# Fused attention and two expert layers on one core: scores and probabilities x values of neighbouring tiles in one group on TensorE, the eight transposes in another, in turns 8 to 21

## Chip, cores and metric

The kernel runs on one core of a Trainium2 chip. The metric is the time of one execution in device microseconds, as the median of three runs. Engines are written as the profile writes them: PE is TensorE (matmuls; a transpose is a matmul with the identity matrix), PEld its weight loads, DVE VectorE, ACT ScalarE, POOL GpSimd, SP SyncE, which here only issues transfers.

## What is computed

The reference has three parts, one behind the other:

```python
# attention: 4 batches x 8 heads, 768 tokens, 64 per head; chunks of 32 tokens
# that look at 8 memory keys and 16 tokens to the left, 8 to the right
scores = scale * np.matmul(q_c, k_full.transpose(0, 1, 3, 2))
a = np.exp(scores - np.max(scores, axis=-1, keepdims=True))
a = a / (np.sum(a, axis=-1, keepdims=True) + 1e-09)
out[:, :, c_start:c_end] = np.matmul(a, v_full)
# layer 1: x is 3072 x 512, w_in 512 x 1024, w_out 1024 x 512
h = x @ w_in
e = np.exp(h - h_max); sm = e / (np.sum(e, axis=-1, keepdims=True) + 1e-9)
solu = h * sm
ln = (solu - mu) / np.sqrt(var + 1e-06) * g_ln
x2 = ln @ w_out
# layer 2: 512 -> 2048 -> 512
h = x2 @ w_in2; g = np.maximum(0.01 * h, h); return g @ w_out2
```

Weights come as 64-bit floats and are decoded on the chip. Products of layer 1 are made of three: each operand is split into a high and a low half (names that end in `h` and `l`), and high x high, high x low and low x high are added up.

## The kernel before

The 3072 tokens are 24 tiles of 128. After a start written out by hand the loop from line 477 runs turns i = 0 to 24; behind it comes layer 2 (line 715 and around it), which the change leaves as it is. A turn works on several tiles at once, at different stages:

- **Attention of tile a = i + 2.** `s_scores` (S): 16 matmuls of 128x32 column groups (line 208) into a PSUM tile `att`; each such group shows as 32 instructions in the trace. Then the negated row maxima `nms` on DVE (lines 217, 218; in the first and the last tile of a batch a memset ahead). `s_exp`: eight exponentials on ACT (line 225), one a head, into `p`. `s_pt` (PT): four transposes of `p` (line 238) into a PSUM tile `tr`, copied out by DVE as `pt` (line 242). `s_pv` (PV): 16 matmuls probabilities x values (line 250) into another `att`, scaled out by DVE as `x` (line 255). `x_halves` (XT): four transposes of `x` (line 264), then `xh` on ACT (line 267) and `xl` on DVE (line 270).
- **Layer 1, first half, of tile i.** `s_h`: 24 matmuls "h" (line 284) of 128x512 into PSUM `h`, then a chain between DVE and ACT: `hnm` (DVE, line 297), `e` (ACT, the exponential of line 300), `hrs` (DVE, 301 and 302), `so` and `nmu` (DVE, 305 and 308), the square (ACT, line 310), `ve` (DVE 311), `rstd` (POOL 313) and the normalized `so` (DVE 318).
- **Its transposition, of tile i - 1.** `s_lt` in turns 7 to 22: two DVE transposes of 32x32 blocks into `sl` (line 337), a store to DRAM (`lnd`, SP's queue), four loads back issued by ACT (`lt`, line 346), and two copies each on ACT and DVE into the halves `lhl` (lines 354, 355).
- **Layer 1, second half, of tile i - 5.** `s_o`: 24 matmuls of 128x512 into PSUM `x2p` (line 366, "products" below), copied out by ACT as `x2s` (line 374) and stored by ACT's queue. Turn 7 takes three blocks.
- **Decoding of layer 2's weights** from turn 9 on: per turn one `abs` on ACT (line 112), four steps on DVE (lines 114 to 127), and every second turn four more DVE operations on `w3s` (lines 470 to 473).

`p` and `x` have one buffer, `att` and `tr` two, `h` one. Except in the start, the order of instructions on each engine is that of the tile framework's scheduler: it places S, PT, PV and XT between the h matmuls and the products where it thinks their inputs are ready. Each engine then runs its own list strictly in that order, and waits at semaphores.

Of the kernel before, what the change touches and what calls it, by code (L numbers as in the profile page):

```python
# [33 lines left out]
ON_POOL = range(6)  # L34

SPARE_PSUM = (1, 3, 5)

F64_LO = struct.unpack("<f", struct.pack("<I", 0x38000000))[0]
F64_HI = struct.unpack("<f", struct.pack("<I", 0x47EFFFFF))[0]
# [3 lines left out]
def tile_kernel(  # L43
# [14 lines left out]
    NTILE = qt.shape[0]  # L58
# [38 lines left out]
    def load_raw(src, pool):  # L97
        raw = pool.tile([P, 512, 2], U32, name="raw")
        if len(src.shape) == 2:
            nc.sync.dma_start(out=raw.rearrange("p f w -> p (f w)"), in_=src)  # L100
        else:
            nc.sync.dma_start(out=raw.rearrange("p (k f) w -> p k (f w)", k=src.shape[1]), in_=src)
        return raw
# [39 lines left out]
    def decode(raw, dh, dl, pool, gain=None, sub=nc.gpsimd):  # L143
        for _ in decode_steps(raw, dh, dl, gain, pool, sub):
            pass
        return lows[-1]
# [24 lines left out]
    def kv_tile(pool, name, eng):  # L171
        t = pool.tile([P, 2, 4, 4, 64], F32, name=name)
        eng.memset(t[:, 0], 0.0)
        eng.memset(t[:, 1], 0.0)
        return t
# [3 lines left out]
    kbd = kv_tile(p1, "kbd", nc.vector)  # L179
    vbd = kv_tile(p1, "vbd", nc.vector)  # L180

    def load_q(i):
        q = pa.tile([P, 4, P], F32, name="q")
        nc.sync.dma_start(out=q, in_=qt[i].rearrange("p (h t) -> p h t", h=4))
        return q

    def load_kv(i, dst, src):
        for j in range(2):
            nc.sync.dma_start(
                out=dst[j::2, j], in_=src[i, j::2].rearrange("p (h c k) -> p h c k", h=4, c=4)  # L190
            )
        return dst

    def load_tile(i):
        return load_q(i), load_kv(i, kbd, kw), load_kv(i, vbd, vw)

    def load_w2(kk):
        decode(
            load_raw(w2[kk * P : (kk + 1) * P, :], dec), w2h[:, kk], w2l[:, kk],
            dec, g_sb[:, kk : kk + 1],  # L200
        )

    def s_scores(i, q, k):
        sc = ps_att.tile([P, 8, 64], F32, name="att")
        for hp in range(4):
            for c in range(4):
                cs = slice(32 * c, 32 * c + 32)
                nc.tensor.matmul(  # L208
                    sc[cs, 2 * hp : 2 * hp + 2, :], q[:, hp, cs], k[:, :, hp, c, :],
                    start=True, stop=True,  # L210
                )
        if i % TPB == 0:
            nc.vector.memset(sc[0:32, :, 8:24], NEG)
        if i % TPB == TPB - 1:
            nc.vector.memset(sc[96:128, :, 56:64], NEG)
        nms = sm.tile([P, 8], F32, name="nms")
        nc.vector.tensor_reduce(out=nms, in_=sc, op=ALU.max, axis=AX.X, negate=True)
        nc.vector.tensor_scalar_mul(nms, nms, SCALE)  # L218
        return sc, nms

    def s_exp(sc, nms):
        p = p1.tile([P, 4, 64, 2], F32, name="p")
        rs = sm.tile([P, 8], F32, name="rs")
        for h in range(8):
            nc.scalar.activation(  # L225
                p[:, h // 2, :, h % 2], sc[:, h], AF.Exp, bias=nms[:, h : h + 1], scale=SCALE,
                accum_out=rs[:, h : h + 1],
            )
        return p, rs

    def s_rs(rs):
        nc.vector.tensor_scalar_add(rs, rs, 1e-9)
        nc.vector.reciprocal(rs, rs)

    def s_pt(p):
        ptp = ps_tr.tile([P, 4, P], F32, name="tr")
        for hp in range(4):
            nc.tensor.transpose(  # L238
                ptp[:, hp], p[:, hp].rearrange("p k j -> p (k j)"), ident
            )  # L240
        pt = pa.tile([P, 4, P], F32, name="pt")
        nc.vector.tensor_copy(pt, ptp)
        return pt

    def s_pv(pt, v, rs):
        xp = ps_att.tile([P, 8, 64], F32, name="att")
        for hp in range(4):
            for c in range(4):
                cs = slice(32 * c, 32 * c + 32)
                nc.tensor.matmul(  # L250
                    xp[cs, 2 * hp : 2 * hp + 2, :], pt[:, hp, cs], v[:, :, hp, c, :],
                    start=True, stop=True,
                )
        x = p1.tile([P, 8, 64], F32, name="x")
        nc.vector.tensor_tensor(
            out=x, in0=xp, in1=rs.unsqueeze(2).to_broadcast([P, 8, 64]), op=ALU.mult
        )
        return x

    def s_xt(x):  # L260
        xtp = ps_tr.tile([P, 4, P], F32, name="tr")
        xf = x.rearrange("p h k -> p (h k)")
        for kk in range(KD):
            nc.tensor.transpose(xtp[:, kk], xf[:, kk * P : (kk + 1) * P], ident)  # L264
        xh = pa.tile([P, KD, P], F32R, name="xh", bufs=3)
        xl = pa.tile([P, KD, P], F32R, name="xl", bufs=3)
        nc.scalar.activation(xh, xtp, AF.Copy)

        def low():
            nc.vector.tensor_tensor(out=xl, in0=xtp, in1=xh.bitcast(F32), op=ALU.subtract)  # L270

        return (xh, xl), low

    def x_halves(x):
        hl, low = s_xt(x)
        low()
        return hl
# [122 lines left out]
    ENG = mybir.EngineType  # L400
# [52 lines left out]
    ld = load_tile(3)  # L453
# [7 lines left out]
    def store_w3(f, m):  # L461
        w3m.append(m.bitcast(F32))
        a = m.bitcast(F32).rearrange("p (k f) -> p k f", k=2)
        if f % 2 == 0:
            nc.sync.dma_start(out=w3f[f // 2, :, 0:2], in_=a)
            return
        s = p2.tile([P, 3, 256], F32, name="w3s")
        b = w3m[-2].rearrange("p (k f) -> p k f", k=2)
        tt = nc.vector.tensor_tensor
        tt(out=s[:, 0], in0=a[:, 0], in1=a[:, 1], op=ALU.add)  # L470
        tt(out=a[:, 0], in0=b[:, 0], in1=a[:, 0], op=ALU.subtract)
        tt(out=s[:, 1], in0=s[:, 0], in1=b[:, 0], op=ALU.subtract)
        tt(out=s[:, 2], in0=b[:, 1], in1=s[:, 1], op=ALU.subtract)
        nc.sync.dma_start(out=w3f[f // 2, :, 2:4], in_=a)
        nc.sync.dma_start(out=w3f[f // 2, :, 4:7], in_=s)

    for i in range(NTILE + 1):
        a = i + 2
        b, t = divmod(i, TB)
        if i < NTILE and t == 0:  # L480
            lhl = lp.tile([P, 2, KF, BT], F32R, name="lhl")
            lb[b] = (lhl[:, 0], lhl[:, 1])
        att = 2 < a < NTILE
        if att:
            p, rs = s_exp(*s_scores(a, ld[0], ld[1]))
            s_rs(rs)
        nso = None
        if i == max(SPARE_PSUM) + 1:
            sx2.close()
            ps_x2 = sx2.enter_context(tc.tile_pool(name="ps_x2b", bufs=2, space=PSUM, side="right", reuse_waits="tile"))  # L490
        if i == NTILE - 1:
            sps.close()
            ps_h2 = sps.enter_context(tc.tile_pool(name="ps_h2", bufs=1, space=PSUM, reuse_waits="tile"))
            spare = ps_h2.tile([P, DFF], F32, name="h2")
        if i < NTILE:
            if i < 2:
                nso = s_h(None, hs[i], True)
            else:
                nso = s_h(xs.pop(0), spare if i in (*SPARE_PSUM, NTILE - 1) else None, i in ON_POOL)
        if att:  # L500
            pt = s_pt(p)
        if so is not None:
            j = i - 1
            s_lt(so, j // TB, j % TB, *lb[j // TB])
        so = nso
        if att:
            x = s_pv(pt, ld[2], rs)
            if a + 1 < NTILE:
                ld = load_tile(a + 1)
        for kk in W2_AT.get(i, ()):  # L510
            load_w2(kk)
        if w3s is not None:
            store_w3(i - 1 - W3_FROM, w3s)
        if 0 <= i - W3_FROM < KF2:
            f = i - W3_FROM
            raw = load_raw(w3[:, 2 * f * P : 2 * (f + 1) * P].rearrange("(k p) f -> p k f", p=P), dec)
            w3s = decode(raw, None, None, dec)
        js = O_AT.get(i, (i - LAG,) if i >= LAG else ())
        for j in js:
            s_o(j // TB, j % TB, *lb[j // TB], 0)  # L520
            if att and j == js[0]:
                xs.append(x_halves(x))
            s_o(j // TB, j % TB, *lb[j // TB], 1)
        if att and not js:
            xs.append(x_halves(x))

    store_w3(KF2 - 1, w3s)
    sps.close()
# [497 lines left out]
```

## Time and profile before

| what | us |
|---|---|
| median of three runs | 846.62 (846.52 to 846.77) |
| the profiled execution | 845.34 |
| its span in the trace | 843.6 |
| PE busy in it | 824.1 (98%) |
| turns 8 to 21, from the start of S in turn 8 to that in turn 22's place | 206.5 |

[...] A turn is counted from the start of its S on PE: turn 8 begins at 120.59 us, turn 9 at 140.35, turn 10 at 155.18, and turn 21 ends at 327.13. Turn 8 carries 24 products more; the others are alike. Busy time on PE is that of a pipeline: its matmuls overlap, so what one costs is read from the distance between starts and not from its duration. The granted clock of PE is 1.00 of full speed all through these turns.

### The profile page before, as it was taken

The page shows a single profiled execution, that of the slowest core. Times are in us where ns is not written, and L with a number is a line of the kernel's source. Part 1 is how long each engine was busy: PE and PEld are TensorE (multiplying, and loading weights), DVE is VectorE, ACT ScalarE, POOL GpSimd, SP SyncE. Part 2 cuts the span into 40 slices and gives each one's busy share as a digit, 9 for nine tenths or more (in the row PEclk, how much of TensorE's full clock was granted, in tenths as well). Part 3 has the DMA queues.
Part 4 walks back from the last instruction along what each step waited for, and adds up shares of the span by engine and source line. Part 5 has one row for each costly group of instructions (what it writes and reads, how often), then busy time and mean ns, then how long its engine had stood idle before and what let it go on. Part 6 is the DMA issues. An engine that isn't in the chain of part 4 may idle for free.

```text
span 843.6 us, 13753 instructions
## 1 busy us (share of the span) xinstructions
PE 824.1 (98%) x5014; PEld 663.8 (79%) x5014; DVE 644.6 (76%) x1145; ACT 471.1 (56%) x1067; POOL 57.4 (7%) x63
## 2 busy tenths in 40 slices
PE   7899999999999999999999999999999999999998
PEld 6676777777777778887888888888787888888886
DVE  8989986878787778758888855675689678768663
ACT  5587844554555444537555646677657344544541
POOL 3333300000000000000000000000000000010001
PEclk9999999999999999999999999999999999999999
DMA  9555685877777576532889964586696375546542
GB/s 335 198 179 177 202 282 190 264 256 241 251 245 243 182 218 212 214 139 96 309 324 314 328 251 199 196 324 258 242 364 220 124 267 188 196 160 230 189 148 101
DMA packets 69892, 190.97 MB, mean 226 GB/s; under 512 B 8000, under 2 KB 32064, under 8 KB 65856
## 3 DMA queue, kind: packets, MB, share of 16 engines
q1 hardware_dynamic: 56864, 175.14, 58.9%
q10 hardware_dynamic: 12960, 14.95, 5.5%
q8 instruction: 40, 0.66, 0.3%
q14 instruction: 28, 0.23, 0.1%
HBM read 129.24 MB, written 60.82 MB: 225 GB/s over the span
## 4 chain that ended last, share of the span: by engine, by line
PE 86%; DVE 6%; ACT 4%; DMA 2%; POOL 1%; issue 1%; DVEq 0%; ACTq 0%; SPq 0%; POOLq 0%
PE C L715 25%; PE x2p L366 16%; PE B L715 14%; PE h L284 13%; PE A L715 10%; PE att L250 3%; PE att L208 2%; DMA ring<-gd 1%; PE tr L238 1%; PE tr L264 1%; DVE ring L826 1%; ACT p L225 1%; PE x2p L284 1%; DMA kbd<-in_kw 1%; POOL w2l L138 1%
## 5 line engine op out<-in xcount | busy, mean ns | idle before, releaser
L366 PE MATMUL x2p<-lhl,w2h 128*128 128x512 f32 x384 | 126.7, 406 | 0.0
L715 PE MATMUL C<-xP,L 128*128 128x512 f32 x384 | 95.4, 390 | 2.2 <-ACT u L744 1.7
L715 PEld LDWEIGHTS C<-xP,L 128*128 128x128 f32 x384 | 71.9, 188 | 17.9 <-ACT u L744 2.1
L366 PEld LDWEIGHTS x2p<-lhl,w2h 128*128 128x128 f32 x384 | 69.8, 189 | 16.3 <-issue 2.4
L366 PE MATMUL x2p<-lhl,w2l 128*128 128x512 f32 x192 | 77.6, 404 | 0.0
L225 ACT ACTIVATE p<-att,nms 128x64 f32<-128x64 f32 x192 | 57.6, 328 | 25.3 <-DVE nms L218 25.2
L284 PE MATMUL h<-w1h,xh 128*128 128x512 f32 x168 | 69.3, 412 | 0.0
L284 PE MATMUL h<-w1h,xl 128*128 128x512 f32 x168 | 67.0, 399 | 0.0
L715 PE MATMUL C<-h,L 128*128 128x512 f32 x192 | 67.0, 390 | 0.0
L284 PE MATMUL h<-w1l,xh 128*128 128x512 f32 x168 | 66.7, 397 | 0.0
L826 DVE TENSOR_TENSOR ring<-ring,h 128x512 fp32r<-128x512 f32 x96 | 61.9, 686 | 3.8 <-ACT h L825 3.2
L310 ACT ACTIVATE e<-so,nmu 128x1024 f32<-128x1024 f32 x24 | 27.6, 1151 | 58.1 <-DVE nmu L308 54.1
L741 ACT ACTIVATE g<-g 128x512 f32<-128x512 f32 x72 | 45.0, 627 | 23.3 <-DVE g L760 18.6
L825 ACT ACTIVATE h<-ring 128x512 fp32r<-128x512 f32 x72 | 39.8, 621 | 32.3 <-DMA ring<-gd 16.7
L715 PE MATMUL B<-xP,L 128*128 128x512 f32 x192 | 48.9, 390 | 0.2 <-DVE g L770 0.2
L825 ACT ACTIVATE h<-t2k 128x512 fp32r<-128x512 f32 x48 | 28.6, 628 | 34.4 <-DVE t2k L818 19.9
L760 DVE TENSOR_TENSOR g<-B,u 128x512 f32<-128x512 f32 x23 | 15.9, 690 | 36.1 <-PE B L715 36.0
L715 PEld LDWEIGHTS B<-xP,L 128*128 128x128 f32 x192 | 36.0, 188 | 8.1 <-DVE g L770 0.6
L715 PEld LDWEIGHTS C<-h,L 128*128 128x128 f32 x192 | 36.0, 188 | 7.9 <-DVE u L940 0.5
L366 PEld LDWEIGHTS x2p<-lhl,w2l 128*128 128x128 f32 x192 | 36.1, 188 | 7.7 <-issue 0.6
L225 ACT ACTIVATION_READ_ACCUMULATOR p<-att,nms 128x1 f32 x192 | 41.3, 215 | 0.0
L284 PEld LDWEIGHTS h<-w1h,xh 128*128 128x128 f32 x168 | 32.0, 191 | 10.1 <-issue 3.8
(187 smaller groups left out, 1917.9 us busy)
## 6 DMA issues: line engine op xcount, KB each, us to landing
ring<-gd SPq DMA_DIRECT2D x48, 768.0 KB, 4.0
gd<-g SPq DMA_DIRECT2D x24, 1024.0 KB, 4.8
raw<-in_w SPq DMA_DIRECT2D x32, 512.0 KB, 5.0
L<-w3f SPq DMA_DIRECT2D x14, 896.0 KB, 5.0
kbd<-in_kw SPq DMA_DIRECT2D x46, 256.0 KB, 4.4
vbd<-in_vw SPq DMA_DIRECT2D x46, 256.0 KB, 3.6
lnd<-sl SPq DMA_DIRECT2D x16, 512.0 KB, 3.7
lt<-lnd ACTq DMA_DIRECT2D x64, 128.0 KB, 2.8
```

The source lines that it names most:

```text
L138: sub.tensor_tensor(out=dl, in0=m, in1=dh.bitcast(F32), op=ALU.subtract)
L208: nc.tensor.matmul(sc[cs, 2 * hp : 2 * hp + 2, :], q[:, hp, cs], k[:, :, hp, c, :], start=True, stop=True,)
L225: nc.scalar.activation(p[:, h // 2, :, h % 2], sc[:, h], AF.Exp, bias=nms[:, h : h + 1], scale=SCALE, accum_out=rs[:, h : h + 1],)
L250: nc.tensor.matmul(xp[cs, 2 * hp : 2 * hp + 2, :], pt[:, hp, cs], v[:, :, hp, c, :], start=True, stop=True,)
L284: nc.tensor.matmul(h[:, hf * 512 : hf * 512 + 512], a[:, kk], b, start=kk == 0 and j == 0, stop=kk == KD - 1 and j == 2,)
L310: nc.scalar.activation(e, so, AF.Square, bias=nmu, accum_out=ve)
L366: nc.tensor.matmul(ps, a[:, kk, es], r[:, kk], start=(kk == 0 and n == 0), stop=(kk == KF - 1 and n == 2),)
L715: nc.tensor.matmul(acc, w[i], x[j], start=first and n == 0, stop=last and n == 2, skip_group_check=True)
L741: nc.scalar.activation(u.g[:, i], u.g[:, i] if src is None else src, AF.Prelu, alpha=0.01)
L760: tt(out=o.g[:, 1], in0=o.acc["B"], in1=o.u2, op=ALU.add)
L825: nc.scalar.activation(h[:, i], src[n_], AF.Copy)
L826: tt(out=l[:, i], in0=src[n_], in1=h[:, i].bitcast(F32), op=ALU.subtract)
```

## The change

For turns 8 to 21 (`GROUPED`) PE's order is that in which the code is written, and the code is written in another order. The attention of a tile is spread over two turns. A grouped turn i runs on PE: the 24 h of tile i; PV of tile a; directly behind it S of tile a + 1; the 24 products; XT of tile a; and PT of tile a + 1. Turn 7 already ends with S and PT of tile 10. The other engines' orders are still made by the scheduler, and their instructions are the same ones, as many as before. `q` and `k` of a tile are loaded one turn earlier (`load_qk`), and its `v` behind the PV that last read the buffer. Lines move by five.

```diff
+GROUPED = range(8, 22)
...
+    def load_qk(i):
+        return load_q(i), load_kv(i, kbd, kw)
...
+        if i == GROUPED[0]:
+            turns.enter_context(tc.manual_schedule(engines={ENG.PE}))
+        if i == GROUPED[-1] + 1:
+            turns.close()
...
-        if att:
+        grouped = i in GROUPED
+        if att and not grouped:
             p, rs = s_exp(*s_scores(a, ld[0], ld[1]))
             s_rs(rs)
...
-        if att:
+        if grouped:
+            x = s_pv(pt, vbd, rs)
+            if a + 1 < NTILE:
+                load_kv(a + 1, vbd, vw)
+                p, rs = s_exp(*s_scores(a + 1, *ld))
+                if a + 2 < NTILE:
+                    ld = load_qk(a + 2)
+        elif att:
             pt = s_pt(p)
...
-        if att:
+        if att and not grouped:
             x = s_pv(pt, ld[2], rs)
-            if a + 1 < NTILE:
-                ld = load_tile(a + 1)
+            ld = load_tile(a + 1)
...
-            if att and j == js[0]:
+            if att and not grouped and j == js[0]:
                 xs.append(x_halves(x))
             s_o(j // TB, j % TB, *lb[j // TB], 1)
-        if att and not js:
+        if att and (grouped or not js):
             xs.append(x_halves(x))
+        if i + 1 in GROUPED:
+            if not grouped:
+                p, rs = s_exp(*s_scores(a + 1, *ld[:2]))
+                ld = load_qk(a + 2)
+            s_rs(rs)
+            pt = s_pt(p)
```

PE in a middle turn before, from the last h matmul on (`tr<-ident,p` is PT, `att<-vbd,pt` PV, `tr<-ident,x` XT; the S that follows belongs to the next turn):

```order
L284 MATMUL h<-w1h,xl 128x512
L238 MATMUL tr<-ident,p 128x128
L366 MATMUL x2p<-lhl,w2h 128x512 x2
L238 MATMUL tr<-ident,p 128x128
...
L366 MATMUL x2p<-lhl,w2h 128x512
L250 MATMUL att<-vbd,pt 32x128 x16
L366 MATMUL x2p<-lhl,w2h 128x512
...
L264 MATMUL tr<-ident,x 128x128 x4
L366 MATMUL x2p<-lhl,w2h 128x512 x2
...
L208 MATMUL att<-kbd,q 32x128 x16
L284 MATMUL h<-w1h,xh 128x512
```

PE in the same turn of the change, again from the last h matmul to the first of the next turn:

```order
L289 MATMUL h<-w1h,xl 128x512
L255 MATMUL att<-vbd,pt 32x128 x16
L213 MATMUL att<-kbd,q 32x128 x16
L371 MATMUL x2p<-lhl,w2h 128x512 x2
...
L371 MATMUL x2p<-lhl,w2l 128x512
L269 MATMUL tr<-ident,x 128x128 x4
L243 MATMUL tr<-ident,p 128x128 x4
L289 MATMUL h<-w1h,xh 128x512
```

PV and S stand next to each other, all 24 products behind them, and PT has moved from the products' first half to the turn's very end, behind XT.

ACT before, from one turn's exponential `e` of h to the next turn's exponentials of scores (`p,rs<-att,nms`), with the square (`e,ve<-so,nmu`) between them:

```order
L300 ACTIVATE e,hrs<-h,hnm 128x1024
L346 DMA lt<-lnd 32x4x256 x3
L310 ACTIVATE e,ve<-so,nmu 128x1024
L346 DMA lt<-lnd 32x4x256
L267 ACTIVATE xh<-tr 128x512
L374 ACTIVATE x2s<-x2p 128x512
L225 ACTIVATE p,rs<-att,nms 128x64
L375 DMA x2d<-x2s 128x512
L354 ACTIVATE lhl<-lt 128x4x128 x2
L225 ACTIVATE p,rs<-att,nms 128x64 x7
```

ACT in a middle turn of the change (turn 16):

```order
L351 DMA lt<-lnd 32x4x256
L305 ACTIVATE e,hrs<-h,hnm 128x1024
L351 DMA lt<-lnd 32x4x256
L230 ACTIVATE p,rs<-att,nms 128x64 x6
L315 ACTIVATE e,ve<-so,nmu 128x1024
L230 ACTIVATE p,rs<-att,nms 128x64 x2
L351 DMA lt<-lnd 32x4x256 x2
L379 ACTIVATE x2s<-x2p 128x512
L272 ACTIVATE xh<-tr 128x512
L380 DMA x2d<-x2s 128x512
L359 ACTIVATE lhl<-lt 128x4x128 x2
```

The exponentials of the scores now stand around the square of the same turn, six ahead of it and two behind. How many stand behind it differs: five in turn 8, all eight in turn 9, four in turn 11, one in turns 14 and 15, six in turns 19 and 20, two in the others.

DVE in turn 12 of the change, from `hnm` to `nmu`, on which the square waits (`x` is the scaling behind PV, `nms` the maxima of the scores, `m` the decoding):

```order
L302 TENSOR_REDUCE hnm<-h 128x1
L260 TENSOR_TENSOR x<-att,rs 128x512
L116 TENSOR_SCALAR m<-m 128x512
L120 TENSOR_SCALAR m<-m 128x512
L222 TENSOR_REDUCE nms<-att 128x8
L124 SCALAR_TENSOR_TENSOR m<-raw,m 128x512
...
L129 SCALAR_TENSOR_TENSOR m<-raw,m 128x512
L307 RECIPROCAL hrs<-hrs 128x1
L310 SCALAR_TENSOR_TENSOR so,nmu<-h,hrs,e 128x1024
L313 TENSOR_SCALAR nmu<-nmu 128x1
```

The maxima of the next tile's scores and `x` now lie in this stretch; before, the maxima came behind `nmu`.

## Rows read from the trace of the kernel before

**Rows 1.** The page's busy time, with share of the span and instructions.

```profile
PE 824.1 (98%) x5014; PEld 663.8 (79%) x5014; DVE 644.6 (76%) x1145; ACT 471.1 (56%) x1067; POOL 57.4 (7%) x63
```

**Rows 2.** Windows, turn 9, turns 10–20: length; PE, PEld, DVE, ACT, POOL busy; clock.

```profile
140.35:155.18 14.83, 14.76 (x121) 11.04 (x121) 12.58 (x30) 7.17 (x26) 0.99 (x1) 1.00 0.79 258
155.18:312.89 157.71, 157.71 (x1321) 122.55 (x1320) 124.49 (x266) 82.15 (x273) 6.04 (x11) 1.00 0.72 237
```

**Rows 3.** Timeline of PE around turn 14's S: start, duration, instruction.

```profile
212.24 0.39 PE L366 MATMUL x2p<-lhl,w2l 128*128 128x512 f32 x1
212.56 1.08 PE L208 MATMUL att<-kbd,q 128*32 128x128 f32 x32
213.57 0.50 PE L284 MATMUL h<-w1h,xh 128*128 128x512 f32 x1
213.90 0.40 PE L284 MATMUL h<-w1l,xh 128*128 128x512 f32 x1
```

**Rows 4.** Timeline of PE at 102 us, where PV and S stand side by side.

```profile
102.05 0.60 PE L328 MATMUL tr<-ident,so 128*128 128x128 f32 x4
102.58 1.08 PE L250 MATMUL att<-vbd,pt 128*32 128x128 f32 x32
103.47 1.06 PE L208 MATMUL att<-kbd,q 128*32 128x128 f32 x32
104.46 0.50 PE L284 MATMUL h<-w1h,xh 128*128 128x512 f32 x1
104.80 0.40 PE L284 MATMUL h<-w1l,xh 128*128 128x512 f32 x1
```

**Rows 5.** Timeline of PE: a transpose, two products, the next transpose.

```profile
219.16 0.27 PE L238 MATMUL tr<-ident,p 128*128 128x128 f32 x1
...
219.74 0.27 PE L238 MATMUL tr<-ident,p 128*128 128x128 f32 x1
```

**Rows 6.** The chain of waits in turn 8: start, length, what.

```profile
132.78 0.44 PE tr L238 x4
```

**Rows 7.** Timeline in turn 15: the last h matmul, then DVE up to so.

```profile
233.24 0.39 PE L284 MATMUL h<-w1h,xl 128*128 128x512 f32 x1
...
233.67 1.23 DVE L297 TENSOR_REDUCE hnm<-h 128x1 f32<-128x1024 f32 x1
...
236.33 0.42 DVE L114 TENSOR_SCALAR m<-m 128x512 f32<-128x512 f32 x1
...
237.24 0.69 DVE L122 SCALAR_TENSOR_TENSOR m<-raw,m 128x512 uint32<-128x512 uint32 x1
...
237.93 0.67 DVE L255 TENSOR_TENSOR x<-att,rs 128x512 f32<-128x512 f32 x1
238.51 1.27 DVE L305 SCALAR_TENSOR_TENSOR so<-h,hrs,e 128x1024 f32<-128x1024 f32 x1
```

**Rows 8.** Timeline of ACT in turn 15, the square and what follows.

```profile
240.58 1.15 ACT L310 ACTIVATE e<-so,nmu 128x1024 f32<-128x1024 f32 x1 [4.45 <-DVE nmu L308]
...
241.73 0.58 ACT L267 ACTIVATE xh<-tr 128x512 fp32r<-128x512 f32 x1
```

**Rows 9.** Timeline in turn 9: exponentials, and the transpose that waits for one.

```profile
147.36 0.34 ACT L225 ACTIVATE p<-att,nms 128x64 f32<-128x64 f32 x1
...
147.65 0.34 ACT L225 ACTIVATE p<-att,nms 128x64 f32<-128x64 f32 x1
...
147.84 0.33 PE L238 MATMUL tr<-ident,p 128*128 128x128 f32 x1
```

**Rows 10.** Timeline in turn 8: the products' end on PE, the last exponential on ACT.

```profile
128.99 0.39 PE L284 MATMUL h<-w1h,xl 128*128 128x512 f32 x1
...
129.56 0.32 ACT L225 ACTIVATE p<-att,nms 128x64 f32<-128x64 f32 x1
```

**Rows 11.** DMA issues: KB each, median us from issue to landing.

```profile
lnd<-sl SPq DMA_DIRECT2D x16, 512.0 KB, 3.7
lt<-lnd ACTq DMA_DIRECT2D x64, 128.0 KB, 2.8
```

More of the change, by code (lines that the diff above doesn't have):

```diff
@@ L475, in store_w3 @@
         nc.sync.dma_start(out=w3f[f // 2, :, 4:7], in_=s)
+    turns = ExitStack()
     for i in range(NTILE + 1):
```

## The prediction, on record before the changed kernel ran

> **What bounds the kernel now.** I read the page's busy times first: PE works in 98% of the span [rows 1], so an edit pays only by what it takes from PE's row of starts, and costs what it puts there as waiting. Then the windows by turn: in turns 10 to 20 PE is busy for the whole 157.71 us, 14.34 a turn, at full granted clock, while DVE has work for 11.3 us of a turn (124.49 / 11) and ACT for 7.5 [rows 2]. Only turn 9, 14.83 us long, has a gap: 0.5 us over the mean, where PT waits for the exponentials one by one [rows 2, 9]. So before the change PE waits for almost nothing in the turns that change, because the scheduler puts PT, PV and XT where their inputs are already there. What can be gained is what the changes of shape between matmuls cost; what can be lost is that scheduling.
>
> **What grouping saves on PE.** A lone S between a product and an h matmul: the product starts at 212.24, the second h matmul at 213.90, 1.66 us later [rows 3]. Without the S two steps of 0.23 from one matmul's start to the next would lie between them, so a lone group costs 1.66 - 0.46 = 1.20. PV stands alone as well and I take the same. The pair exists once in this trace, behind four transposes: from 102.05 to the second h matmul at 104.80 are 2.75 us; four transposes take 0.44 [rows 6], a product 0.23, and 2.08 is left for the pair [rows 4]. Two lone groups 2.40, a pair 2.08: 0.32 saved a pair. Turns 8 to 20 each get a pair (turn 21 has no next tile): 13 x 0.32 = 4.2 us. A transpose among products costs 0.58 - 0.46 = 0.12 [rows 5], one in a group of four 0.11 [rows 6]; eight in one group instead of two places saves at most one more entrance, and I take 0.04 a turn, 0.5 in all. Turn 9's present gap of 0.5 goes with its place. Together 5.2 us.
>
> The Trainium skill, "TensorEngine Tiling (Array Packing)", Key Properties, says that changing the tiling mode, not just the tile, drains TensorE. Rows 3 and 4 agree: two groups of one mode side by side are 0.32 cheaper than apart. By that rule alone, with nothing waiting, the gain would be the whole 4.2 us of the pairs.
>
> **What grouping makes late.** I count from the start of a turn's last h matmul. PV starts 0.32 later, as S does behind a product (212.24 to 212.56) [rows 3], the first product at 0.32 + (104.46 - 102.58) = 2.20 [rows 4]; 24 products, the first 0.34, the rest 0.23, end at 7.83; XT takes 0.44, and the fourth PT would start at 8.60. PT used to be fed from exponentials made long ago; now the same tile's scores were finished only at about 2.0, and all eight exponentials must be done 0.48 before the last PT (147.36 to 147.84) [rows 9].
>
> ACT's order now has the square of h in front of some of these exponentials, and ACT runs its list in order, so those wait for the whole chain `hnm`, `e`, `hrs`, `so`, `nmu`. When does the square start? From the DVE rows: `hnm` 0.43 behind the last h matmul (233.24 to 233.67), 1.14 long as it spaces the row behind it when nothing waits (1.23 less overlap); then in the new order `x` 0.58, two decode steps 0.45 each (0.42 and a pause), the maxima of the scores 0.6 (same size as `x`), two more decode steps 0.6 each, three small ones 0.4 together; then from the start of `so` to the square 2.07, of which 0.6 is a decode step that stands there before and not now [rows 7, 8]: 0.43 + 1.14 + 0.58 + 0.9 + 0.6 + 1.2 + 0.4 + 1.47 = 6.7. By the turns' own orders I get 5.9 in turn 9 (no decode there), 6.6 in turns 10 and 11, 6.7 in 12, 17 and 18, 6.8 in 13 to 16, 4.8 in 19 and 20.
>
> From the square to the next ACT instruction is 1.15 (240.58 to 241.73) [rows 8], exponentials follow each other by 0.29 (147.36 to 147.65) [rows 9]. With n of them behind the square the last PT can start at square + 1.15 + (n - 1) x 0.29 + 0.48, against 8.60:
> - turn 9, n = 8: 5.9 + 3.66 = 9.6: waits 1.0.
> - turn 11, n = 4: 6.6 + 2.50 = 9.1: waits 0.5.
> - turns 10, 12, 17, 18 with n = 2: 6.6 to 6.7 + 1.92 = 8.5 to 8.6: nothing; 13 and 16: 8.7, 0.1 each.
> - turns 14 and 15, n = 1: 6.8 + 1.63 = 8.46: nothing; 19 and 20, n = 6: 4.8 + 3.08 = 7.9: nothing.
> - turn 8: its PT stands behind the first 24 products, so the fourth could start at 128.99 + 0.33 = 129.32, but the last exponential started at 129.56 [rows 10], which allows 130.04: waits 0.7.
>
> Two turns start late. Turns 13 and 16 hold two decodes and the operations on `w3s`: DVE's mean of 11.3, one more decode (2 x 0.42 + 2 x 0.69, less overlap, 1.9) and half a `w3s` (0.85, four steps of the size of the first) is 14.1 us, in a turn that would last 14.34 - 0.36 = 14.0, and DVE must also pause for `hnm` and `hrs`. I take `hnm` of turns 14 and 17 as 0.5 late: their PT wait 0.4 and 0.5. Sum: 1.0 + 0.5 + 0.2 + 0.7 + 0.9 = 3.3. Of the transfers `lnd` to `lt`, with 3.7 and 2.8 us to landing [rows 11], the copies into `lhl` stand ahead of `hnm` on DVE and ACT; their turn gives them some 5 to 6 us, so some will be late: between 0 and 1 us in all, I take 0.3. **Cost 3.6.** What is behind the waiting PT on PE is the next turn's h, so everything is pushed out by it.
>
> The copy of `pt` has all 24 h matmuls, 5.5 us, ahead of the PV that wants it, and normalized `so` likewise; loads of `q`, `k` and `v` have more than half a turn: these edits cost nothing under that cover, and if one lost it, it would cost what it lacks every turn.
>
> **Sum.** -5.2 + 3.6 = -1.6 us on the profiled execution's 845.34: 843.7. The median of the runs stands 1.28 above that execution, 846.62, so 845.0. Bounds of the terms: the pair's saving between 0.2 (turn-to-turn scatter of 0.1 in rows 3 and 4) and 0.4, so 2.6 to 5.2; the waits between 1.5 (only turns 8, 9) and 5. This case alone spans about -3.2 to -0.2: 843.4 to 846.4.
>
> **Rivals.**
> - *Full gain.* The scheduler's order is only late in turns 8 and 9 or not at all; the waits in front of PT come out as the products' own slack. For: two thirds of the turns are within 0.2 us of on time by my sum. Against: the exponentials behind the square are in the list. -5.2: 841.4; with turns 8 and 9 waiting, 843.1.
> - *Slower: DVE late every turn.* Place: the copies into `lhl` and the decodes in front of `hnm`. `hnm` late makes square, exponentials and PT late, and PT late starts the next turn late, at the same DVE load. It decides once the mean extra wait passes (5.2 - 3.6) / 13 = 0.12 us a turn, about the scatter of my own sum; at 0.4 a turn it costs 5.2: +3.6, 850.2; at 0.25, 848.3. For: DVE has 11.3 of 14.0 us of work, and now sits in PT's loop, with no slack to spare in nine turns. Against: at 79% load it has pauses to catch up in most turns.
> - *No saving.* The pair's 0.32 is that of another place (transposes ahead of it instead of products); only the waits stay, less turn 9's gap: about +2.6, 849.2.
>
> On the second rival: the row is ACT's fixed list with the square ahead of two to eight exponentials. The Trainium skill, "TensorE: Matmul & The Clock Gate", the queue depths in its table, calls the queues of ScalarE and VectorE strictly first in, first out, so that no exponential could overtake a square that waits; the same skill's "TensorEngine Tiling (Array Packing)", PSUM Bottleneck, warns that tiling speeds up TensorE but not the evacuation of PSUM. By these the slower case is the natural one; rows 2 leave 3 us of DVE's turn free against it.
>
> **How the numbers follow.** Chances: mostly given back 0.50, full or nearly full gain 0.18, DVE late 0.24, no saving 0.08. 0.2% of 846.62 is 1.7 us, about what a measurement of this kernel can tell from no change: faster is below 844.9, slower above 848.3. The first case lies a little less than half below 844.9 (0.24) and the rest within; faster is 0.24 + 0.18 = 0.42; the DVE case is above 848.3 from 0.25 a turn on (0.17 of its 0.24), "no saving" nearly all: slower 0.17 + 0.07 = 0.24; the rest, 0.34, the same. For 8 in 10 the range takes the first case, half of the full gain and two thirds of the slower ones: 841.6 to 849.4; the likeliest case's own range is 843.4 to 846.4.
>
> **What would show it.** In the trace of the changed kernel: the pair from the last h matmul to the second product should measure 2.54 (0.32 + 1.88 + 0.34) within 0.1; turns without a wait 13.98 instead of 14.34; PE idle in front of PT, released by ACT's `p`, of 0.7 in turn 8, 1.0 in turn 9, about 0.5 in 11, 14 and 17, and none to speak of in 19 and 20. Layer 2 should not change. Wrong, if PT waits in nearly every turn (then slower), if no turn waits (then near 841.4), or if the pair takes 2.40.

## The result

The change makes the kernel slower: 855.32 us in the median of four runs (853.66 to 856.26) against 846.69; the ratio is 1.0097, 95% interval 1.0083 to 1.0111. The forecast was 845.0 in a range of 841.6 to 849.4. The profiled execution took 856.26 us, 10.9 more than that of before. By stretches: 1.1 of it lie ahead of turn 8, 8.2 in turns 8 to 21 (213.7 us from the first h of turn 8 to that of turn 22; before 205.5), 2.1 in the turns behind them, and layer 2 is 0.5 faster. The first is within what the kernels below scatter by there: in those that leave turns 0 to 7 nearly alone, turn 8's h begins anywhere between 121.3 and 123.2 us.

The page of the changed kernel, busy time, and the chain of waits by engine:

```profile
PE 823.7 (96%) x5014; PEld 669.7 (78%) x5014; DVE 641.6 (75%) x1145; ACT 471.8 (55%) x1067; POOL 56.8 (7%) x63
...
PE 71%; DMA 6%; DVE 4%; ACT 1%; issue 1%; POOL 0%; SPq 0%; ACTq 0%; DVEq 0%; POOLq 0%
```

PE does the same work as before [rows 1] in a longer span. In the chain before, PE had 86% and DMA 2%; now PE has 71% and DMA 6%.

Windows of the changed kernel, from the first h of a turn to the next turn's, turns 12 to 19 (columns as in rows 2):

```profile
186.69:200.59 13.90, 13.90 (x121) 11.44 (x122) 11.78 (x27) 7.65 (x26) 0.28 (x1) 1.00 0.75 240
200.59:215.21 14.62, 14.12 (x123) 11.45 (x122) 12.64 (x28) 8.18 (x27) 0.36 (x2) 1.00 0.81 261
215.21:232.77 17.56, 14.78 (x121) 11.52 (x122) 11.81 (x28) 7.74 (x26) 0.69 (x2) 1.00 0.83 271
232.77:248.25 15.48, 15.48 (x122) 12.58 (x122) 12.33 (x29) 7.91 (x27) 0.66 (x2) 0.89 0.64 214
248.25:264.03 15.78, 14.12 (x124) 11.45 (x121) 12.57 (x27) 7.91 (x27) 0.41 (x2) 1.00 0.73 243
264.03:280.61 16.58, 14.11 (x122) 11.43 (x122) 11.78 (x27) 7.65 (x26) 0.97 (x2) 1.00 0.88 293
280.61:296.10 15.49, 15.49 (x121) 12.57 (x122) 12.10 (x27) 7.67 (x26) 0.42 (x2) 0.89 0.50 170
296.10:309.98 13.88, 13.88 (x123) 11.45 (x122) 10.30 (x21) 7.29 (x26) 0.81 (x2) 1.00 0.64 225
```

A turn without a wait takes 13.88 us, 0.46 less than before [rows 2]: the gain is there, and a little more than forecast. It is lost in single turns: 0.7 in turn 13, 3.7 in turn 14, 1.9 in 16, 2.7 in 17, where PE is less busy than the window is long. Turns 15 and 18 lose 1.6 each in another way: PE is busy all the time, but at 0.89 of its clock.

Where the pair stands, here in turn 13 (timeline of PE), it costs what it did in rows 4. From the last h matmul to the second product it takes 2.54 us, as forecast:

```profile
205.90 0.39 PE L289 MATMUL h<-w1h,xl 128*128 128x512 f32 x1
206.22 1.08 PE L255 MATMUL att<-vbd,pt 128*32 128x128 f32 x32
207.12 1.06 PE L213 MATMUL att<-kbd,q 128*32 128x128 f32 x32
208.11 0.73 PE L371 MATMUL x2p<-lhl,w2h 128*128 128x512 f32 x2
```

Now turn 14. What SP issued at the end of turn 13 and in the beginning of turn 14 (timeline, SP's queue):

```profile
214.34 0.33 SPq L470 DMA_DIRECT2D w3f<-m  x1
214.76 1.09 SPq L104 DMA_DIRECT2D raw<-in_w  x2
218.61 0.34 SPq L347 DMA_DIRECT2D lnd<-sl  x1
```

Turn 13 decodes twice, which frees two `raw` buffers, so two loads of 512 KB start together 3.9 us ahead of the store `lnd`. The view of that store's DMA issue:

```profile
lnd<-sl SPq DMA_DIRECT2D x1, 512.0 KB, 7.6
```

7.6 us to landing; the median before was 3.7 [rows 11]. ACT in turn 14 (timeline):

```profile
222.17 0.70 ACT L114 ACTIVATE m<-raw 128x512 f32<-128x512 f32 x1 [3.86 <-DMA raw<-in_w]
226.28 0.31 ACTq L351 DMA_DIRECT2D lt<-lnd  x1
226.64 1.12 ACT L305 ACTIVATE e<-h,hnm 128x1024 f32<-128x1024 f32 x1 [3.77 <-DMA lnd<-sl]
...
231.09 1.15 ACT L315 ACTIVATE e<-so,nmu 128x1024 f32<-128x1024 f32 x1 [0.30 <-DVE nmu L313]
...
232.23 0.30 ACT L230 ACTIVATE p<-att,nms 128x64 f32<-128x64 f32 x1
```

ACT stands 3.77 us idle. What it waits for is no input of its own: the next instruction in its list is the issue of a load `lt`, which may start only when the store has landed, and behind it in the list stands `e`, the exponential of h, whose input `hnm` began on DVE at 221.41. So `e` is late, then `so`, the square, and the one exponential of the scores behind the square. The seven ahead of the square are late too, by way of DVE: the last step of their maxima (`nms`, line 223) stands there behind `hrs`, which waits for `e`, and runs only at 228.35:

```profile
228.35 0.15 DVE L223 TENSOR_SCALAR nms<-nms 128x8 f32<-128x8 f32 x1
```

PE at the same place:

```profile
228.31 0.60 PE L269 MATMUL tr<-ident,x 128*128 128x128 f32 x4
229.36 0.33 PE L243 MATMUL tr<-ident,p 128*128 128x128 f32 x1 [0.45 <-ACT p L230]
...
232.67 0.33 PE L243 MATMUL tr<-ident,p 128*128 128x128 f32 x1 [1.81 <-ACT p L230]
232.77 0.47 PE L289 MATMUL h<-w1h,xh 128*128 128x512 f32 x1
...
233.85 0.63 PE L289 MATMUL h<-w1l,xh 128*128 128x512 f32 x1
234.28 0.63 PE L289 MATMUL h<-w1h,xl 128*128 128x512 f32 x1
...
236.84 0.51 PE L289 MATMUL h<-w1h,xl 128*128 128x512 f32 x1
```

PT, placed last, waits to 232.67, and from 233.85 to 236.84 the h matmuls of turn 15 start 0.43 apart instead of 0.23. The windows of the stall and of that stretch:

```profile
229.00:232.67 3.67, 0.98 (x3) 0.42 (x3) 2.12 (x6) 3.37 (x18) 0.02 (x1) 1.00 0.86 247
233.85:236.84 2.99, 2.99 (x9) 2.31 (x7) 2.73 (x7) 0.00 (x0) 0.00 (x0) 0.50 0.81 272
```

The granted clock is 0.50, the lower of the two levels (1.2 GHz instead of 2.4), after a stretch in which PE worked for only 0.98 of 3.67 us. Turn 16 repeats the stall behind a store that took 6.2 us, turn 17 behind one that took 6.3 and had two raw loads ahead of it again. Turn 13 has a short one of the same kind: the store landed at 208.68, the `lt` behind it was issued at 208.75, and `e` began at 209.12, 0.9 after ACT was free.

### The profile page after: what moved, and what is told of

The parts are those of the page before. It is cut to its first block, busy times and chain, and to the rows that moved or that the text cites. A ratio compares the mean times of both kernels' runs of the same rounds, so it can differ in the third digit from the quotient of the medians.

```text
span 854.5 us, 13763 instructions
## 1 busy us (share of the span) xinstructions
PE 823.7 (96%) x5014; PEld 669.7 (78%) x5014; DVE 641.6 (75%) x1145; ACT 471.8 (55%) x1067; POOL 56.8 (7%) x63
## 4 chain that ended last, share of the span: by engine, by line
PE 71%; DMA 6%; DVE 4%; ACT 1%; issue 1%; POOL 0%; SPq 0%; ACTq 0%; DVEq 0%; POOLq 0%
PE C L738 26%; PE B L738 15%; PE A L738 11%; PE h L289 8%; PE x2p L371 8%; DMA lnd<-sl 2%; DMA kbd<-in_kw 1%; PE att L255 1%; PE att L213 1%; DMA L<-w3f 1%; DMA lt<-lnd 1%; DMA x2d<-x2s 1%; DVE so L310 1%; PE tr L243 0%; DVE sl L342 0%
## 5 line engine op out<-in xcount | busy, mean ns | idle before, releaser
L371 PE MATMUL x2p<-lhl,w2h 128*128 128x512 f32 x384 | 120.8, 395 | 0.0
L371 PE MATMUL x2p<-lhl,w2l 128*128 128x512 f32 x192 | 75.1, 391 | 0.0
L230 ACT ACTIVATE p<-att,nms 128x64 f32<-128x64 f32 x192 | 57.5, 328 | 16.7 <-DVE nms L223 12.7
L305 ACT ACTIVATE e<-h,hnm 128x1024 f32<-128x1024 f32 x21 | 23.5, 1121 | 60.2 <-DVE hnm L302 41.0
L289 PEld LDWEIGHTS h<-w1h,xl 128*128 128x128 f32 x168 | 32.7, 195 | 9.3 <-DVE xl L275 2.2
```

Source lines behind the costliest of these rows:

```text
L230: nc.scalar.activation(p[:, h // 2, :, h % 2], sc[:, h], AF.Exp, bias=nms[:, h : h + 1], scale=SCALE, accum_out=rs[:, h : h + 1],)
L289: nc.tensor.matmul(h[:, hf * 512 : hf * 512 + 512], a[:, kk], b, start=kk == 0 and j == 0, stop=kk == KD - 1 and j == 2,)
L305: nc.scalar.activation(e, h, AF.Exp, bias=nm, accum_out=rs)
L371: nc.tensor.matmul(ps, a[:, kk, es], r[:, kk], start=(kk == 0 and n == 0), stop=(kk == KF - 1 and n == 2),)
```

## The experiments

Theory A: ACT stands at an `lt` issue for a store that lands late, with `e` behind it. Theory B is the slower rival of the prediction: DVE is over-full, above all where two decodes fall into one turn. Each kernel ran beside runs of before, whose medians are 846.42 for one_raw, lt_on_sp, act_by_hand and pair_amid_products, 846.03 for no_dve_decode, lt_on_pool, split_pair and eight_amid, and 845.77 for grouped_13 and grouped_10.

**one_raw**: the raw loads of the turns left out; one tile is loaded once and decoded again in every turn.

```diff
+    one = None
...
-            raw = load_raw(w3[:, 2 * f * P : 2 * (f + 1) * P].rearrange("(k p) f -> p k f", p=P), dec)
+            raw = one if one is not None else load_raw(w3[:, 2 * f * P : 2 * (f + 1) * P].rearrange("(k p) f -> p k f", p=P), dec)
+            one = raw
             w3s = decode(raw, None, None, dec)
```

> The changed kernel with one raw tile of w3 loaded once and decoded every turn, so that the 512 KB loads of the turns are left out (their data is wrong; all else stays). Theory A with its cause in the queues (lnd lands late, 6 to 7.6 us instead of 3.7, because raw loads run beside it): lands within 5, 846 to 851 us. Theory A with another cause for the late store, or theory B: 853 to 857.

844.11 us, 0.9974 (0.9964 to 0.9984) of before: 11 us less than the change, further than expected. The stores land in 2.6 to 3.9 us in turns 9 to 20, `e` is nowhere held by them in these turns, PT waits 0.7 us in all by the view of waits, and the clock does not fall. Its order has other double decodes. Those of turns 11, 14 and 17 cost at most 0.3 us each; behind one in turn 8, turn 9 loses 1.4 us, where the change loses 1.0 without one. That is against theory B and for the loads on the queue, though not proof of it, since without the loads the decoding itself can start earlier.

**no_dve_decode**: the decoding's DVE steps left out, the loads kept.

```diff
         nc.scalar.activation(m, raw.bitcast(F32)[:, :, 1], AF.Abs, scale=65536.0)
         yield
+        if dh is None:
+            return
         nc.vector.tensor_scalar(
```

> The changed kernel without the four VectorE steps of the decoding of w3 (left out, layer 2 gets wrong weights); all loads and stores stay. Theory B: with 2 us less VectorE work a turn all waits of turns 14 to 18 go; 842 to 845 us. Theory A: the 512 KB loads still run beside the store lnd, which only leaves some 1 to 2 us earlier; part of the waits stays: 847 to 853.

844.14 us, 0.9969 (0.9956 to 0.9982): as theory B had it, and lower than A's 847 to 853. The trace says why A was wrong about this run: the store of tile 13 leaves 11.0 us behind the last h matmul instead of 12.7, and no raw load stands beside it, since with the early decodes the loads come one at a time, at another point of the turn:

```profile
214.32 0.33 SPq L349 DMA_DIRECT2D lnd<-sl  x1
219.13 0.38 SPq L104 DMA_DIRECT2D raw<-in_w  x1
```

So the run relieves both conditions, and does not tell A from B. One wait for a transfer is left without any decode: in turn 13 DVE stands 3.3 us for a copy into `lhl`, with `hnm` behind it, and the turn loses 1.3. The next two take the wait off ACT and leave loads and decodes.

**lt_on_pool** and **lt_on_sp**: the loads `lt` of turns 8 to 21 issued by another engine.

```diff
-            nc.scalar.dma_start(
+            (nc.gpsimd if TB * b + t + 1 in GROUPED else nc.scalar).dma_start(
```

> The changed kernel with the lt loads of turns 8 to 21 issued by GpSimd, whose only other work there is rstd. Theory A (the exponential of h stands behind an lt issue that waits for the store lnd): the stall leaves ScalarE, PT waits in turns 14, 16 and 17 shrink from 3.6, 1.8 and 2.6 us to under 1; 845 to 850 us, unless rstd behind the same wait takes its place. Theory B (VectorE over-full): 853 to 857.

850.09 us, 1.0054 (1.0037 to 1.0071), just above the expected range: 4.1 over its runs of before, where the change is 8.6 over its own. POOL now does the standing, 39.2 us for `lnd` by its view of waits. `e` begins 1.7 to 2.2 us behind the last h matmul in every turn but turn 11, and the losses of turns 14, 16 and 17 go from 3.7, 1.9 and 2.7 to 1.2, 0 and 0. In turn 11 the transfers are late in another place: the fourth `lt` stands on POOL behind `rstd`, DVE waits 3.0 us for a copy into `lhl` ahead of `hnm`, and 2.4 us are lost, with 1.6 more at half clock in turn 12. Its order has several double decodes, two of them in turns 13 and 14, one behind the other. These two turns, in windows:

```profile
204.66:219.49 14.83, 14.36 (x124) 11.49 (x122) 12.86 (x26) 8.00 (x27) 3.25 (x5) 1.00 0.93 305
219.49:234.59 15.10, 14.56 (x122) 11.48 (x122) 14.62 (x34) 8.29 (x27) 3.13 (x5) 1.00 0.90 302
```

0.95 and 1.2 over 13.88, with `e` on time, and with DVE busy for 14.62 of 15.10. But this is not the price of DVE's load: the square begins 6.6 and 6.0 us behind the last h, as in turns of the change without a wait for PT (6.3 to 6.6 in turns 10, 12, 15 and 18), and five and eight exponentials stand behind it, for which the prediction's own sum gives 0.8 and 1.1. Whether the double decode put them there, by way of the orders, is not shown. In the change the double decode of turn 13 comes with losses of 0.7, 3.7 and 1.6 in turns 13 to 15, that of turn 10 with none in its own turn and the 0.7 in turn 11 that four exponentials behind the square explain. So theory A is the larger part, and of theory B no run shows a price of its own.

> The loads lt of turns 8 to 21 are issued by SyncE instead of ScalarE. Theory A (ScalarE stands at an lt issue that waits for the store lnd, with the exponential of h behind it, 3.8, 2.4 and 3.3 us in turns 14, 16 and 17): these stalls go, the 11.2 us that TensorE waits in turns 14 to 18 fall under 3; 844 to 849 us. Theory B (VectorE is over-full where two decodes fall into one turn): nothing changes, 853 to 857.

871.53 us, 1.0295 (1.0279 to 1.031): much slower, so the expectation failed, although what it rested on came true: PT waits 2.6 us instead of 8.5 and `e` begins 1.7 us behind the last h in every turn from the ninth on. SP stands at the same place, and now the stores, loads and further `lt` of all tiles queue behind it. The products wait for `lhl`:

```profile
206.06 1.06 PE L213 MATMUL att<-kbd,q 128*32 128x128 f32 x32
213.34 0.80 PE L371 MATMUL x2p<-lhl,w2h 128*128 128x512 f32 x1 [6.23 <-ACT lhl L359]
```

Every fourth turn opens a block of products that needs the tile transposed in the turn before; a late `lt` has no slack there. Behind this stall too the granted clock is 0.50, for 8 us.

**act_by_hand**: ACT's order written out as well.

```diff
-            turns.enter_context(tc.manual_schedule(engines={ENG.PE}))
+            turns.enter_context(tc.manual_schedule(engines={ENG.PE, ENG.Activation}))
...
+        if later is not None:
+            later.append((so, nmu, e))
+            return so
+        return s_norm(so, nmu, e, early)
```

(`s_norm` is the part of `s_h` from the square on, called behind `s_exp` and `s_lt`; the copies into `lhl` stand at the turn's end.)

> ScalarE's order in turns 8 to 21 is written out too: exponential of h, all eight exponentials of the scores, the four lt loads, the square. Theory A: no exponential stands behind the square or behind a load, so PT waits nowhere but at the entry in turn 8; 840.5 to 844 us. Theory B: VectorE still late in turns 14 and 17; 848 to 853.

893.36 us, 1.0553 (1.0535 to 1.0571). A miss: the exponentials did go out early (PT waits at most 0.4 us at a time), but DVE's order was made anew around ACT's, and puts `xl`, a decode and both `lhl` copies ahead of `hrs`, so `so` starts 9.6 us behind `hnm` (201.03 to 210.60) where the change needs 4.8 (206.33 to 211.16). PE waits 15.3 us for `lhl`, and in front of h matmuls 9.8 behind DVE's `rs` and 3.2 behind `so`. Nothing about A or B follows; it shows that ACT's order can't be fixed here without DVE's.

**grouped_13** and **grouped_10**: the stall under another order of the same work (grouped_10 has `range(10, 22)`).

```diff
-GROUPED = range(8, 22)
+GROUPED = range(13, 22)
```

> The changed kernel with GROUPED from turn 13 on instead of 8. Its order puts the two double decodes into turns 15 and 18 (13 and 16 in the change). If a double decode is what sets off the stall (late store lnd, ScalarE standing at the lt issue of the next turn), TensorE stalls for about 3 us in turns 16 and 19 and at half clock after that, and not in 14 and 17: 852 to 856 us. If the stalls belong to those tiles or to loads at that time: still in 14 and 17. If grouped turns were late by their number alone, 8 instead of 13 pairs: 850 to 852.

848.62 us, 1.0030 (1.0020 to 1.0041): under the expected 852 to 856. The stall moved as expected, from turn 14 to 16: there ACT stands 3.05 us for `lnd`, whose store took 6.6 us, and `e` begins 5.2 us behind the last h. But PT loses only 0.4 in that turn, because this order has all eight exponentials ahead of the square in turn 16. Behind the other double decode, in turn 18, no raw load is left, the store took 2.7 us and turn 19 is on time. A double decode alone does not make the stall. The entry into the new order costs too: in turn 13 PV waits 1.8 us for `pt`.

> The changed kernel with GROUPED from turn 10 on. The waits of turns 8 and 9 (0.7 and 1.0) go, and two pairs (0.46 each) with them; the double decodes stay in turns 13 and 16 and so do the stalls behind them: 853 to 856 us, against 855.3 for the change. If the early waits made the later ones: 846 to 850.

852.85 us, 1.0082 (1.0065 to 1.0098): a little under the expected 853 to 856, and near it in part by luck, since only one of the two expected stalls came and PV waits 2.2 us for `pt` at the entry, in turn 10, which was not expected. This run has the contrast within one trace. SP behind the double decode of turn 13, and then behind that of turn 16:

```profile
216.26 1.37 SPq L104 DMA_DIRECT2D raw<-in_w  x1
218.92 0.32 SPq L347 DMA_DIRECT2D lnd<-sl  x1
...
257.58 1.12 SPq L104 DMA_DIRECT2D raw<-in_w  x2
261.43 0.34 SPq L347 DMA_DIRECT2D lnd<-sl  x1
```

and the DMA issue views of the two stores:

```profile
lnd<-sl SPq DMA_DIRECT2D x1, 512.0 KB, 4.1
...
lnd<-sl SPq DMA_DIRECT2D x1, 512.0 KB, 7.2
```

With one raw load ahead the store takes 4.1 us, `e` of turn 14 begins 3.1 us behind the last h, and turn 14 takes 13.88. With two it takes 7.2, ACT stands for 3.57, and turn 17 takes 17.4 and is followed by half clock:

```profile
268.66 0.31 ACTq L351 DMA_DIRECT2D lt<-lnd  x1
269.02 1.12 ACT L305 ACTIVATE e<-h,hnm 128x1024 f32<-128x1024 f32 x1 [3.57 <-DMA lnd<-sl]
```

Turn 14 has all eight exponentials ahead of the square here, turn 17 only six.

**pair_amid_products**: the pair kept, PT taken out of the late place. PE runs h, PT of tile a, twelve products, PV and S, twelve products, XT.

```diff
-        if grouped:
-            x = s_pv(pt, vbd, rs)
...
-        elif att:
+        if grouped:
+            s_rs(rs)
+        if att:
             pt = s_pt(p)
...
             s_o(j // TB, j % TB, *lb[j // TB], 0)
+            if grouped:
+                x = s_pv(pt, vbd, rs)
+                if a + 1 < NTILE:
+                    load_kv(a + 1, vbd, vw)
+                    p, rs = s_exp(*s_scores(a + 1, *ld))
...
```

> Pair kept, but amid the products (12 ahead, 12 behind), and PT behind the 24 h matmuls, so that the exponentials have some 8.5 us instead of 6. Theory A: a late exponential of h no longer reaches PT; what is left is the saving of the pairs, 0.46 us a turn: 840 to 843. Theory B: late VectorE delays so and with it the next h: 844 to 848. If the pair saved nothing: 846 to 847.

840.13 us, 0.9925 (0.9911 to 0.9940), within theory A's range. In turns 9 to 20 no turn is more than 0.14 us over its shortest. Neither cause is left in its trace, though: PT has its time, and `e` begins 1.7 to 2.4 us behind the last h in turns 8 to 21, with no double decode among them. It shows the gain without the waits, not which of their conditions was worth what. A turn:

```profile
154.99:168.96 13.97, 13.97 (x123) 11.40 (x122) 12.26 (x27) 7.93 (x30) 0.49 (x1) 1.00 0.70 222
```

**split_pair**: as pair_amid_products, with S at the turn's end.

```diff
-                    p, rs = s_exp(*s_scores(a + 1, *ld))
...
+        if grouped and a + 1 < NTILE:
+            p, rs = s_exp(*s_scores(a + 1, *ld))
```

> As pair_amid_products, but S stands alone at the turn's end instead of next to PV. If the pair saves what rows 3 and 4 of before say, 0.32 us in each of 13 turns: 844.3, between 843.5 and 845.5. If what pair_amid_products gained came from elsewhere: 839.5 to 841.

849.28 us, 1.0034 (1.0020 to 1.0047), above the expected 843.5 to 845.5: the split cost more than the pair. A turn without a wait:

```profile
156.59:170.89 14.30, 14.30 (x124) 11.37 (x120) 11.51 (x29) 7.60 (x25) 0.55 (x1) 1.00 0.77 242
```

14.30 against 13.97: 0.33 a pair, 4.3 in 13. Of the other 5 us 3.1 are waits, since from the end of S to PT there are now only 5.6 us and in five turns PT is 0.2 to 0.8 late, as it was in turn 9 of before; 1.8 lie behind the start of turn 23.

**eight_amid**: as pair_amid_products, with XT of the tile before next to PT.

```diff
+        if held is not None:
+            xs.append(x_halves(held))
+            held = None
         if grouped:
             s_rs(rs)
...
+        if grouped and att:
+            held = x
```

> As pair_amid_products, but XT of the tile before stands next to PT, behind the h matmuls, so that the eight transposes are one group again as in the change, with the exponentials' 8.5 us kept. A turn took 13.97 us in pair_amid_products and 13.88 in an undisturbed turn of the change; 13 x 0.09 = 1.2 off: 838.9, between 838 and 839.8. If a late x or late exponentials make the group wait: 840 or more.

839.19 us, 0.9923 (0.9905 to 0.9941), in the expected range: the fastest kernel here, 6.8 us below the runs of before beside it. Its turn takes 13.88, like an undisturbed one of the change. From pair_amid_products the medians differ by 0.9, within what either scatters; that the eight transposes in one group are worth it is read from the turns, 13.88 to 13.97.

## Why the prediction was wrong

- **The saving of the pair** was right: 0.32 forecast from rows 3 and 4, 0.33 measured by split_pair. The eight transposes gained twice what was put down (0.09 instead of 0.04 a turn), so an undisturbed turn is 13.88 and not 13.98. With turn 9's gap the gain is some 6.4, not 5.2.
- **The waits for the exponentials behind the square** were right in place and size: 0.7 in turn 8 and 1.0 in turn 9 (forecast 0.7 and 1.0), 0.7 in turn 11 (0.5), none in turns 10, 12, 19 and 20. `hnm` of turns 14 and 17 is 0.45 late (0.5). The row for turn 9 of the changed kernel: square 154.48, last exponential 157.65, last PT 158.13, as 1.15 + 7 x 0.29 + 0.48 has it.
- **The term that failed** is "of the transfers `lnd` to `lt` ... some will be late: between 0 and 1 us in all, I take 0.3". Measured, turns 13, 14, 16 and 17 lose 9.0 us, of which the forecast had 1.1 under DVE, and the half clock behind two of them costs 3.2, for which the sum had no term. Two things were wrong in that step. It looked at the copies into `lhl` ahead of `hnm`, which cost little in the change (`hnm` begins at most 0.9 us behind the last h), and not at the issue of `lt`, which the order puts ahead of `e` on ACT. Before, all four issues stood behind `e` in turns 9 to 21 except 17 and 18, three of them at a point where ACT had nothing to do but wait for `nmu` [rows 8]. The trace of before showed the wait in turn 17, where `e` began 0.8 late and PE lost nothing (timeline of ACT):

```profile
264.06 0.31 ACTq L346 DMA_DIRECT2D lt<-lnd  x1
264.42 1.12 ACT L300 ACTIVATE e<-h,hnm 128x1024 f32<-128x1024 f32 x1 [2.15 <-DMA lnd<-sl]
```

  And the step priced landing by the median [rows 11], while the orders of SP and DVE put raw loads ahead of just the stores that `e` of these turns stood behind: two for turns 14 and 17, one for turns 13 and 16.
- **The slower rival** had the right sign and the wrong mechanism: DVE is not late every turn. `hnm` begins 0.4 to 0.9 us behind the last h matmul in turns 9 to 21. The prediction also put double decodes into turns 13 and 16 only; turn 10 holds one as well, and takes 13.88.
- **Its sums.** Turns 14 and 15 give 6.8 + 1.63 = 8.43 and not 8.46, with no effect. The stated bounds of the terms (saving of the pairs 2.6 to 5.2, waits 1.5 to 5) add up, with the other 1.0 of gain, to -4.7 to +1.4, more than the -3.2 to -0.2 taken for the likeliest case; the measured +8.6 lies outside either.
- By theory A turn 14 adds up: the store left at 218.61 and landed 7.6 later, at 226.2; `e` had its input from 222.6 on (221.41 and 1.2 for `hnm`). With the median landing of 3.7 the store would have been there at 222.3, and nothing would have stood. The store's late issue, 12.7 us behind the last h of turn 13 instead of 11.7 behind those of turns 12 and 15, comes from DVE's list and is the part of theory B in it.
- What stays open: how much of the 1.1 us ahead of turn 8 and the 2.1 behind turn 21 belongs to the change. The second part is one wait, 2.1 us of PE for the last tile's `so`; the chain there runs over a load of layer 2 (`L<-w3f`) that took 5.9 us to land. Before has no such wait, most of the kernels above have 0.6 to 2.0. ACT also stands 6.9 us for a store in turn 22, but that turn takes 11.0 against 10.9 before. It was not tried apart. Open too is why the stores landed late: raw loads ahead go with it (last section), and no run takes away the loads and leaves all else.

The Trainium skill, "TensorE: Matmul & The Clock Gate", the queue depths in its table, calls ScalarE's queue strictly first in, first out. The trace agrees: `e` had its input from 222.6 us on and began at 226.64, behind a DMA issue. The prediction used that rule for the square and overlooked it for the load.

## What to carry to other kernels

A DMA issue is an instruction in its engine's list: if its source is a store that may land late, everything behind it waits, so put it behind the work that others are waiting for, or see what has to land first. When work is moved to the end of a stage to make groups, list everything ahead of its inputs on every engine, issues included, and take the longest landing under the queue's load, not the median. Here the grouping was worth its 6 us as soon as the group that needs late inputs stood where they were long there.

## What the runs showed of the hardware

- After a stall PE ran at half clock: 0.50 for 3 us behind 3.67 us with 0.98 of work (turn 15 of the change, and again in turn 18), 1.6 us each time on top of the stall. Turn 16's stall of 1.8 us was not followed by it, the clock stayed at 1.00. The length of a wait alone does not decide: in lt_on_pool two waits of PT in turn 11, 1.7 us together, were followed by 0.50, in grouped_10 one wait of 2.2 us in turn 10 was not. The Trainium skill, "TensorE: Matmul & The Clock Gate", states the two levels; which of them follows which stall is read here from the rows.
- The 512 KB store `lnd` landed in 2.6 to 5.1 us where no 512 KB load `raw` had been issued on the same queue within 4 us ahead of it, in 4.1 to 6.6 behind one and in 6.3 to 7.6 behind two (before, change, grouped_10 and grouped_13, turns 9 to 20). In other kernels one with none ahead took 5.7 (split_pair) and one behind a single load 3.6 (lt_on_pool), so the groups overlap. In turn 22 it took 6.6 to 6.8 behind two loads `xt` of 512 KB issued up to 1.7 us ahead (change, one_raw, grouped_10 and grouped_13).
